# A retention kernel's K and Q: cast by the load, or loaded as fp32 and cast on ScalarE

## The chip, the cores and the metric

The kernel runs on one core of one Trainium2 chip. The metric is the device time of one execution in microseconds (us); lower is better. TensorE is called PE, its weight loads PEld, VectorE DVE, ScalarE ACT, GpSimd POOL and SyncE SP, as in the profile.

## The reference

Two layers run one after the other: a retention layer (attention without softmax, with a decay), and a feed-forward layer with a sigmoid-approximated GELU.

```python
# q, k, v: (8, 8, 576, 64) fp32; w_in (512, 2048), w_out (2048, 512)
scores = q @ k.T / sqrt(64)                        # per batch and head
Dmat   = where(i >= j, gamma_h ** (i - j), 0)      # gamma_h = 1 - 2 ** (-5 - h)
ret    = (scores * Dmat) @ v
x      = ret.transpose(0, 2, 1, 3).reshape(4608, 512)
h      = x @ w_in
out    = (h * sigmoid(1.702 * h)) @ w_out
```

## The kernel before

The 4608 tokens are cut into 36 units of 128 rows (all 8 heads of a unit at once), and four units make a chunk; there are nine chunks, 0 to 8. The last 64 rows of two batches share a unit (8, 17, 26, 35), and the loads of such a unit are two DMAs in place of one.

For each unit the kernel needs four things. Its K and Q rows lie in `kqn` as bf16: the DMA on POOL's queue reads fp32 from memory and writes bf16 (`load_kq`, line 228). The same rows lie transposed in `kqT`, made either by PE with an identity (`transpose_pe`, line 360, and a copy out of PSUM by DVE or ACT, line 376) or by a DMA transpose on SP's queue (`dma_transpose`, line 399). Its V rows lie in `vn` as fp32 (`load_v`, line 244) and are scaled into `vp` as bf16 by DVE or POOL (`scale_v`, line 353). PE then computes the scores from `kqT` (line 501), masks go in on the way out of PSUM (`scores_out`, line 514), and a running K-V state per head is added up (`state_both` and `state_sum`, lines 429 and 442), cast on ACT (`cast_range`, line 459) and used for all earlier rows (`inter`, line 476). `ahead(j)` (line 892) issues the scores and states of units 2j and 2j+1; `block(j)` (line 908) issues the rest of the retention for units 2j and 2j+1 and calls `ahead(j + 1)` in its middle.

The feed-forward layer works chunk by chunk in two stages. The up stage multiplies by w_in and applies the GELU on ACT. The down stage multiplies by w_out. From chunk 1 on the down stage, and from chunk 2 on most of the up stage, uses seven products in place of eight, with sums prepared on DVE (classes `Pair` and `UpSet`). A down stage alternates between two PSUM banks A and B: seven products, each emptied by an ACT copy (line 699) or a DVE addition (line 702), with a hook after each product. The retention of later units is fitted into these hooks and between the up products. In the up stage, the two banks are emptied by GELUs or copies on ACT.

All order is written out by hand. An engine executes its instructions in the order in which the program issues them, and `op` (line 41) adds semaphore waits from the names that an instruction reads and writes. The strings `UP` (line 865) and `DOWN` (line 868) give the order of chunks 3 to 7: in `UP`, `@` starts block(2c+2) and `V` issues four `scale_v` on POOL; in `DOWN`, the parts between bars are the seven hooks, and `c` is the cast of the state. `lead_in` (line 959) is chunk 0; the dictionary `work` in it hangs retention steps behind the steps of chunk 0's down stage, which run in the order (0,0), (1,0), (0,1), ... (1,3), (2,0), ... (3,3). `steady` (line 1080) holds chunks 1 to 8.

Units 0 to 7 are transposed on PE, units 8 to 35 by DMA. The DMA transposes are issued in groups at the start of a chunk, and the loads of later units wait for the last of them:

```python
for u in range(10, 14):
    load(u)
for u in range(8, 14):
    dma_transpose(u, [f"vn{13 % NVN}"])
for u in (14, 15):
    load(u, after=[f"T{13 % NQT}_0"])
```

There are 12 tiles `kqn`, 10 tiles `vn`, and 8 each of `kqT` and `vp`; a unit u uses number u modulo that count.

Of the kernel before, what the change touches and what calls it, by code (L numbers as in the profile page):

```python
# [13 lines left out]
P = 128  # L14
# [146 lines left out]
def bass_retnet_parallel__then__act_gelu_quick_kernel(  # L161
# [7 lines left out]
):  # L169
    NLD, NVN, NVP, NQT, NKV, NST = 12, 10, 8, 8, 16, 4  # L170
    es = ExitStack()
    with es:
# [5 lines left out]
        iota_k = sb("iota_k", [P, 5], FP32)  # L178
        kqn = [sb(f"kqn{i}", [P, 2, H, DH], BF16) for i in range(NLD)]
        vn = [sb(f"vn{i}", [P, H, DH], FP32) for i in range(NVN)]  # L180
        w_in_sb = sb("w_in_sb", [P, 4, FF], BF16)
# [45 lines left out]

        def load_kq(u, which, eng="pool", after=()):
            if which and u in RUNS:
                return load_q_runs(u)  # L230
            sl = u % NLD
            src = (k, q)[which]

            def f(e):
                return [
                    e.dma_start(  # L236
                        kqn[sl][p0 : p0 + n, which, :, :],
                        src[b, :, s0 : s0 + n, :].rearrange("h p d -> p h d"),
                    )
                    for p0, n, b, s0 in unit_rows(u)  # L240
                ]
            op(eng, f, reads=after, writes=[f"kq{sl}_{which}"], dma=f"d_kq{sl}_{which}", ndma=len(unit_rows(u)))

# [534 lines left out]
        class UpSet:  # L778
# [85 lines left out]

        UP = """PE13 00 01 V 10 PK12 11 02 12 03 13 04 14 F0 05 F1 20 06 15 16 21 @ L1 x 22 23 L0 F2
            PX14 s2 24 25 PY15 26 L2 g0-8a s2 g8-16a"""

        DOWN = """s2|c g8-16b|B g0-8b s4||x|X|c s2"""
        last_store = {}
# [61 lines left out]
        def cast_now():  # L931
            now(casts)
            casts.clear()

        def load(u, after=()):
            if u < NU:
                load_kq(u, 0, after=after)
                load_kq(u, 1, after=after)
                load_v(u, after=after)
# [19 lines left out]
        def lead_in():  # L959
# [14 lines left out]
            for i in range(4):  # L974
                load_wout(i)
            for u in range(4, 10):
                load(u)
            op("dve", lambda e: e.memset(warmt.ap(), 0.0), writes=["warm"])
# [56 lines left out]
            up_group(0, 0, 4, 2, 3, "A")  # L1035
            scale_v(3)
            scores(3)
            scores_out(3, 1, 0)
# [13 lines left out]
            for f in range(8, NF):  # L1052
                up(0, f)
            def ahead45():
                ahead(2)
                for u in (4, 5):
                    state_sum(u, 0)
                    state_sum(u, 1)
                state_cast(4, 6)
                scores_out(4, 2, 0)  # L1060
                scores_out(4, 2, 1)

            work = {
                (1, 3): lambda: (scale_v(4), transposes(4, "E", "D", "dve")),
                (2, 0): lambda: (transposes(5, "E", "D", "dve"), scale_v(5)),
                (2, 1): ahead45,
                (3, 1): lambda: now(block(2, lambda: None)),
                (3, 2): lambda: (transposes(6, "C", "D", "dve"), scale_v(6)),
                (3, 3): lambda: (transposes(7, "E", "K", "dve"), scale_v(7)),
            }  # L1070
# [9 lines left out]
        def steady():  # L1080
            four = Pair(0, 2, 2)
            for c in range(1, NCH):
                if c == 1:
                    for u in range(10, 14):
                        load(u)
                    for u in range(8, 14):
                        dma_transpose(u, [f"vn{13 % NVN}"])
                    for u in (14, 15):
                        load(u, after=[f"T{13 % NQT}_0"])
                else:  # L1090
                    for u in range({2: 16, 3: 20}.get(c, 4 * c + 6), min(4 * c + 10, NU)):
                        dma_transpose(u)
                    if c == 2:
                        for u in (16, 17):
                            scale_v(u, "pool")
                    if c == 2 or c == NCH - 1:
                        for u in range(4 * c + 10, 4 * c + 14):
                            load(u, after=[f"T{(4 * c + 9) % NQT}_0"])
                last = c == NCH - 1
                if c == 1:  # L1100
                    for i in range(16):
                        f0, lo = 2 * (i % 8), 2 * (i // 8)
                        up_group(1, f0, 2, lo, lo + 2, turn())
                        if i == 0:
                            ahead(3)
                            now(ahead_out(3, False))
# [13 lines left out]
                        if i == 9:  # L1120
                            winsums(0, 8)
                    for u in (14, 15):
                        dma_transpose(u)
                    for u in (16, 17):
                        load(u, after=[f"T{15 % NQT}_0"])
                else:
# [10 lines left out]
                    def side(w, c=c, sums=sums):  # L1137
# [4 lines left out]
                        elif w[0] == "g":  # L1142
                            sums(*[int(f) for f in w[1:-1].split("-")], which=(0, 1) if w[-1] == "a" else (2, 3))
                        elif w == "c":
                            cast_now()
                        elif w == "X":
                            now(xsums(c + 1))
                        elif 2 * (2 * c + 2 + (w == "B")) < NU:
                            rest.extend(block(2 * c + 2 + (w == "B")))
# [5 lines left out]
                    if wide:  # L1155
                        free = "AB" if turns[0] % 2 else "BA"
                        sets.append(UpSet(c, 2, *free))
                        for w in UP.split():
# [4 lines left out]
                            elif w == "V":  # L1163
                                for u in range(4 * c + 6, min(4 * c + 10, NU)):
                                    scale_v(u, "pool", [sets[0].o])
                                for u in range(4 * c + 10, 4 * c + 14):
                                    load(u, after=[f"T{(4 * c + 9) % NQT}_0"])
                            elif w[0] == "L":
# [5 lines left out]
                    else:  # L1174
                        for n in range(7):
                            for w in sets:
                                w.step(n)
                            if c == 2 and n == 1:
                                now(rest)
                                rest.clear()  # L1180
                            if n in ((3, 4) if c == 2 else (1, 4)):
                                for u in vps[:1]:
                                    scale_v(u)
                                del vps[:1]
                            if c == 2 and n == 4:
                                state_cast(12, 14)
                            if n in (4, 5):
                                for w in sets[:-1] if n == 4 else sets[-1:]:
# [37 lines left out]
                def hook(i):  # L1226
                    if c == 1:
# [18 lines left out]
                        if i == 6:  # L1246
                            rest.extend(block(5, cast=False))
                            now(rest[:2] + xsums(2) + rest[6:])
                            rest[:] = rest[2:6]
                        return  # L1250
                    if wide:
# [10 lines left out]
                    if c == 2 and i == 1:  # L1262
                        for u in (18, 19):
                            dma_transpose(u)
                        for f0, f1 in ((0, 8), (8, 12), (12, 16)):
# [11 lines left out]
                    if i == 5:  # L1277
                        now(rest)
                        rest.clear()

                four.run(c, hook)
# [63 lines left out]
```

## Time and profile before

| | |
|---|---|
| median of 3 runs | 280.83 us (280.28 to 280.91) |
| the profiled execution's own time | 282.98 us |
| its span, first to last instruction | 281.0 us |
| mean granted PE clock | 0.994 |
| PE busy | 268.7 us (96%) |
| DVE busy | 201.4 us (72%) |
| ACT busy | 155.6 us (55%) |
| POOL busy, issue of DMAs included | 130.8 us (47%) |
| DMA queue of POOL, share of 16 engines | 71.2% |
| DMA queue of SP, share of 16 engines | 27.7% |

Busy time is summed within an engine, so engines overlap. A matmul counts as busy until its modelled end, and matmuls are pipelined. Where the profile names an instruction, `out<-in` are the tiles that it writes and reads, with L and a line number of the kernel; an idle time is put down to the instruction whose semaphore came last. A DMA has an issue on a queue, whose length is that of the issue, and a landing, which is counted from the start of the issue. Times inside the execution are counted from the start of the span.

### The profile page before, as it was taken

The numbers are of one execution on the slowest core, as the hardware profiler recorded it, in microseconds if no ns is written. First come the engines' busy times: TensorE is split into PE (matmuls) and PEld (weight loads), VectorE is DVE, ScalarE is ACT, GpSimd is POOL, SyncE is SP. The second block draws the span as 40 slices with busy tenths as digits, with TensorE's granted clock in tenths as the row PEclk, the third lists the DMA queues.
The fourth block names the chain that finished last, engine by engine and source line by source line (L and its number), as shares of the span: only waits on it lengthen the run. The fifth ranks groups of instructions, "written<-read, shape, count | busy, mean of one in ns | idle before, by whom it ended". The sixth has DMA issues, their size and how long they took to land.

```text
span 281.0 us, 9605 instructions
## 1 busy us (share of the span) xinstructions
PE 268.7 (96%) x4242; PEld 210.9 (75%) x4262; DVE 201.4 (72%) x397; ACT 155.6 (55%) x276; POOL 130.8 (47%) x161
## 2 busy tenths in 40 slices
PE   7899999999999999969999999998989999999996
PEld 6576355888877688858977887787778977888585
DVE  5863657598698899639867986796679868866551
ACT  7556433754248733846188608850877178608821
POOL 9999979200344769417738914780347020000000
PEclk9999999999999999979999999999999999999999
DMA  9999999998499979998998989794779070003013
GB/s 159 188 204 207 200 221 249 253 168 152 83 162 223 180 57 162 178 225 100 195 268 97 156 113 249 93 199 65 229 76 149 5 211 16 2 2 150 0 45 106
DMA packets 116937, 40.73 MB, mean 145 GB/s; under 512 B 104096, under 2 KB 110240, under 8 KB 116896
## 3 DMA queue, kind: packets, MB, share of 16 engines
q0 software_dynamic: 79712, 22.82, 71.2%
q1 hardware_dynamic: 36896, 17.05, 27.7%
q8 instruction: 33, 0.54, 0.8%
q10 hardware_dynamic: 288, 0.26, 0.3%
q14 instruction: 8, 0.07, 0.1%
HBM read 36.70 MB, written 9.44 MB: 164 GB/s over the span
## 4 chain that ended last, share of the span: by engine, by line
PE 74%; DMA 10%; POOL 8%; DVE 5%; issue 2%; ACT 1%; POOLq 0%
PE psB L686 17%; PE psA L686 17%; DMA vn<-in_v_dram 6%; DMA kqT<-kqn 4%; PE psX L802 4%; PE psC L802 3%; PE psB L580 3%; PE psA L580 3%; PE psB L802 3%; PE psA L802 3%; POOL w_in_sb L271 3%; PE psY L802 2%; PE psD L802 2%; PE psE L566 2%; PE psK L566 2%
## 5 line engine op out<-in xcount | busy, mean ns | idle before, releaser
L236 POOL DMA_DIRECT2D kqn<-in_k_dram x39 | 34.9, 904 | 45.3 <-DMA kqT<-kqn 43.2
L355 POOL TENSOR_TENSOR vp<-vn,vfac 128x512 bf16<-128x512 f32 x20 | 20.5, 1041 | 54.0 <-DVE part L816 43.0
L249 POOL DMA_DIRECT2D vn<-in_v_dram x40 | 36.7, 929 | 0.1
L236 POOL DMA_DIRECT2D kqn<-in_q_dram x37 | 33.1, 904 | 0.6 <-issue 0.6
L825 ACT ACTIVATE gT<-part 128x512 bf16<-128x512 f32 (+1 forms) x38 | 30.6, 847 | 0.0
L699 ACT ACTIVATE osb<-psA 128x512 f32<-128x512 f32 (+1 forms) x19 | 10.5, 552 | 35.6 <-PE psA L686 35.5
L699 ACT ACTIVATE osb<-psB 128x512 f32<-128x512 f32 (+1 forms) x17 | 9.3, 547 | 33.1 <-PE psB L686 33.1
L460 ACT ACTIVATE kv<-stm 128x1024 bf16<-128x1024 f32 (+1 forms) x17 | 15.3, 901 | 10.7 <-DVE stm L451 10.7
L554 DVE TENSOR_TENSOR xT<-psX,gq 128x512 bf16<-128x512 f32 x16 | 11.0, 689 | 14.0 <-PE psX L529 14.0
L686 PE MATMUL psA<-wsum,gT 128*128 128x256 bf16 x144 | 17.4, 273 | 0.1
L686 PE MATMUL psB<-wsum,part 128*128 128x256 bf16 x128 | 15.6, 273 | 1.0 <-issue 1.0
L686 PE MATMUL psA<-wsum,part 128*128 128x256 bf16 x128 | 15.5, 273 | 0.0
L686 PEld LDWEIGHTS psA<-wsum,gT 128*128 128x128 bf16 x144 | 13.9, 98 | 2.1 <-DVE osb L702 0.4
L686 PE MATMUL psA<-w_out_sb,gT 128*128 128x256 bf16 x128 | 15.4, 273 | 0.0
L686 PE MATMUL psB<-w_out_sb,gT 128*128 128x256 bf16 x128 | 15.4, 273 | 0.0
L668 DVE TENSOR_TENSOR part<-gT 128x1024 bf16<-128x1024 bf16 (+2 forms) x20 | 11.6, 580 | 4.9 <-ACT gT L825 4.3
L580 PE MATMUL psB<-xT,w_in_sb 128*128 128x256 bf16 x112 | 14.6, 273 | 0.0
L686 PEld LDWEIGHTS psB<-wsum,part 128*128 128x128 bf16 x128 | 12.3, 98 | 2.7 <-issue 1.2
L355 DVE TENSOR_TENSOR vp<-vn,vfac 128x512 bf16<-128x512 f32 x16 | 10.6, 685 | 4.7 <-DMA vn<-in_v_dram 4.7
L686 PEld LDWEIGHTS psB<-w_out_sb,gT 128*128 128x128 bf16 x128 | 12.5, 98 | 1.9
L816 DVE TENSOR_TENSOR part<-psY,part 128x512 f32<-128x512 f32 x14 | 9.6, 687 | 5.9 <-ACT part L812 4.0
L580 PE MATMUL psA<-xT,w_in_sb 128*128 128x256 bf16 (+1 forms) x120 | 13.8, 259 | 0.0
(186 smaller groups left out, 749.1 us busy)
## 6 DMA issues: line engine op xcount, KB each, us to landing
vn<-in_v_dram POOLq DMA_DIRECT2D x32, 256.0 KB, 5.7
out_dram<-osb SPq DMA_DIRECT2D x30, 256.0 KB, 2.6
kqn<-in_k_dram POOLq DMA_DIRECT2D x31, 128.0 KB, 5.0
kqn<-in_q_dram POOLq DMA_DIRECT2D x31, 128.0 KB, 5.6
w_out_sb<-in_moe_w_out_dram POOLq DMA_DIRECT2D x4, 512.0 KB, 13.8
out_dram<-osb SPq DMA_DIRECT2D x10, 128.0 KB, 2.3
w_in_sb<-in_moe_w_in_dram POOLq DMA_DIRECT2D x8, 128.0 KB, 5.3
w_in_sb<-in_moe_w_in_dram POOLq DMA_DIRECT2D x4, 256.0 KB, 7.8
```

The lines of the kernel that those rows point to most:

```text
L236: e.dma_start(kqn[sl][p0 : p0 + n, which, :, :], src[b, :, s0 : s0 + n, :].rearrange("h p d -> p h d"),)
L249: e.dma_start(vn[sl][p0 : p0 + n, :, :], v[b, :, s0 : s0 + n, :].rearrange("h p d -> p h d"))
L355: op(eng, lambda e: e.tensor_tensor(vp[u % NVP].ap(), vn[sl].ap(), vfac[:, ty, :, None].to_broadcast([P, H, DH]), ALU.mult), reads=[f"vn{s ...
L460: op("act", lambda e: e.activation(kv[:, i0 % NKV : i0 % NKV + n, :, :], stm[:, i0 % NST : i0 % NST + n, :, :], AF.Copy), reads=[f"stm{(i0 ...
L554: op("dve", lambda e: e.tensor_tensor(xT[ch % 2][:, slice(hh, 4, 2), P * jj : P * jj + 2 * P].rearrange("p g (u t) -> p u g t", u=2), ps32 ...
L566: op("pe", lambda e, a=a: e.matmul(bank[b][:, n0:n1], w_in_sb[:, a, P * f : P * f + P], xT[c % 2][:, a, n0:n1], start=(a == 0), stop=(a == ...
L580: op("pe", lambda e, a=a, f=f, i=i: e.matmul(bank[b][:, n * i : n * i + n], w_in_sb[:, a, P * f : P * f + P], xT[c % 2][:, a, P * lo : P * ...
L668: op("dve", lambda e, d=d, x=x, y=y, alu=alu: e.tensor_tensor(d, x, y, alu), reads=kx + ky, writes=kd)
L686: op("pe", lambda e, x=x, y=y, t=t, s=not more and t == 0 and k == 0, z=k == NF // 2 - 1: e.matmul(bank[b][:, 256 * t : 256 * t + 256], x, ...
L699: op("act", lambda e: e.activation(dst[0], src[0], AF.Copy), reads=src[1], writes=dst[1])
L802: op("pe", lambda e, x=x, y=y, i=i, s=not more and i == 0 and k == 0, z=k == 1: e.matmul(bank[b][:, 256 * i : 256 * i + 256], x, y, start= ...
L825: op("act", lambda e: e.activation(dst, src, AF.Gelu_apprx_sigmoid), reads=reads, writes=[f"g_{f0 + 2 * i + q}_{j}" for i in range(2) for ...
```

## The change

K and Q of units 4 to 35 are loaded as fp32 into four staging tiles `stage`, still on POOL's queue, and a new `cast_kq` casts them on ACT into `kqn`. Units 0 to 3 stay as they were. Except for units 4 and 5, which PE still transposes, each cast issues the unit's DMA transpose right behind itself, so units 6 and 7 are now transposed by DMA too, and no group of DMA transposes is left. With the staging tiles, `kqn` shrinks from 12 to 8 tiles and `vn` from 10 to 6. K and Q loads and V loads of one unit are issued apart from each other at many places, and no load waits for a DMA transpose any more; a K or Q load waits for the cast that empties its staging tile. In chunk 0, `ahead45` moves from behind step (2,1) to behind (2,2), and in chunk 1 `ahead(3)` moves from behind the first of 16 `up_group`s to behind the second. In chunks 3 to 7 the casts of the next chunk but one's units stand at the hooks (`k1` to `k4`), and the loads stand in the up stage (`l1`, `l2`, `v`); `l1` has a wait for the DVE instruction issued last before it.

```diff
-    NLD, NVN, NVP, NQT, NKV, NST = 12, 10, 8, 8, 16, 4
+    NLD, NVN, NSG, NVP, NQT, NKV, NST = 8, 6, 4, 8, 8, 16, 4
...
+        stage = [sb(f"stage{i}", [P, 2, H, DH], FP32) for i in range(NSG)]
...
-        def load_kq(u, which, eng="pool", after=()):
+        def load_kq(u, which, eng="pool", after=(), gate=()):
...
-            sl = u % NLD
             src = (k, q)[which]
+            if u < 4:
+                dst, key = kqn[u], f"kq{u}_{which}"
+            else:
+                dst, key = stage[u % NSG], f"sg{u % NSG}_{which}"
...
+        def cast_kq(u, which=(0, 1), on_pe=False):
+            if u >= NU:
+                return
+            n = slice(which[0], which[-1] + 1)
+            op("act", lambda e: e.activation(kqn[u % NLD][:, n, :, :], stage[u % NSG][:, n, :, :], AF.Copy),
+               reads=[f"sg{u % NSG}_{i}" for i in which], writes=[f"kq{u % NLD}_{i}" for i in which])
+            if which[-1] and not on_pe:
+                dma_transpose(u)
...
-        UP = """PE13 00 01 V 10 PK12 11 02 12 03 13 04 14 F0 05 F1 20 06 15 16 21 @ L1 x 22 23 L0 F2
+        UP = """PE13 l1 00 01 V 10 PK12 11 02 12 l2 v 03 13 04 14 F0 05 F1 20 06 15 16 21 @ L1 x 22 23 L0 F2
...
-        DOWN = """s2|c g8-16b|B g0-8b s4||x|X|c s2"""
+        DOWN = """s2|c g8-16b k1|k2 B g0-8b s4|k3|x k4|X|c s2"""
...
+        def loads(u, gate=()):
+            if u < NU:
+                load_kq(u, 0, gate=gate)
+                load_kq(u, 1, gate=gate)
...
-            for u in range(4, 10):
-                load(u)
+            load(4)
+            load(5)
+            for u in (6, 7):
+                loads(u)
...
+            for u in range(6, 10):
+                load_v(u)
...
-                (1, 3): lambda: (scale_v(4), transposes(4, "E", "D", "dve")),
-                (2, 0): lambda: (transposes(5, "E", "D", "dve"), scale_v(5)),
-                (2, 1): ahead45,
+                (1, 3): lambda: (scale_v(4), load_v(10), cast_kq(4, on_pe=True), loads(8)),
+                (2, 0): lambda: (cast_kq(5, on_pe=True), loads(9), transposes(4, "E", "D", "dve")),
+                (2, 1): lambda: (transposes(5, "E", "D", "dve"), scale_v(5), load_v(11)),
+                (2, 2): lambda: (cast_kq(6), loads(10), cast_kq(7), loads(11), ahead45()),
                 (3, 1): lambda: now(block(2, lambda: None)),
-                (3, 2): lambda: (transposes(6, "C", "D", "dve"), scale_v(6)),
-                (3, 3): lambda: (transposes(7, "E", "K", "dve"), scale_v(7)),
+                (3, 2): lambda: (scale_v(6), load_v(12)),
+                (3, 3): lambda: (scale_v(7), load_v(13)),
...
+            HOOK1 = ((12,), (13,), (), (14,), (15,), (16,), ())
+            CASTS = (3, 4, 7, 8, 11, 12)
...
-                if c == 1:
-                    for u in range(10, 14):
-                        load(u)
-                    for u in range(8, 14):
-                        dma_transpose(u, [f"vn{13 % NVN}"])
-                    for u in (14, 15):
-                        load(u, after=[f"T{13 % NQT}_0"])
-                else:
-                    for u in range({2: 16, 3: 20}.get(c, 4 * c + 6), min(4 * c + 10, NU)):
-                        dma_transpose(u)
...
-                        if i == 0:
+                        if i == 1:
                             ahead(3)
                             now(ahead_out(3, False))
...
+                        if i == 0:
+                            cast_kq(8)
+                            loads(12)
+                        if i in CASTS:
+                            cast_kq(9 + CASTS.index(i) // 2, (CASTS.index(i) % 2,))
+                        if i == CASTS[1]:
+                            loads(13)
+                    for u in range(14, 16):
+                        load(u)
...
+                            elif w[0] == "l":
+                                for u in range(4 * c + 8 + 2 * int(w[1]), 4 * c + 10 + 2 * int(w[1])):
+                                    loads(u, [pr.streams["dve"][-1]] if w == "l1" else ())
+                            elif w == "v":
+                                for u in range(4 * c + 10, min(4 * c + 14, NU)):
+                                    load_v(u)
...
                             if c == 2 and n == 1:
                                 now(rest)
                                 rest.clear()
+                                cast_kq(17)
+                                for u in (16, 17):
+                                    scale_v(u, "pool", [sets[0].o])
+                                load(18)
+                                load(19)
...
                             if c == 2 and n == 4:
                                 state_cast(12, 14)
+                                load(20)
+                                load(21)
...
+                    if c == 2 and i in (1, 2, 3, 4):
+                        cast_kq(17 + i)
```

`range(6, 10)` stands in `lead_in` behind `scale_v(3)`. `HOOK1` holds the units that chunk 1's seven hooks cast, `CASTS` the up_groups of chunk 1 that are followed by half a cast (K or Q) of units 9 to 11. In chunk 1's hooks the casts of units 12 and 13 are followed by the loads of K and Q of units 16 and 17, and the cast of 13 also by the V loads of 16 and 17.

## The prediction

> **What bounds the kernel now.** I read the page's busy shares and slices first, then the waits, then the stretches of the trace stage by stage.
>
> ```profile
> PE 268.7 (96%) x4242; PEld 210.9 (75%) x4262; DVE 201.4 (72%) x397; ACT 155.6 (55%) x276; POOL 130.8 (47%) x161
> ...
> PEclk9999999999999999979999999999999999999999
> DMA  9999999998499979998998989794779070003013
> ```
>
> PE is busy 96% of 281.0 us: the kernel is its matmul stream, and time is won or lost only where that stream shrinks or stands still. DMA is loaded in the first 150 us. One clock slice is low, about 119 to 126 us. The list of waits has one PE wait of size, and the stretches show what it cost (stretch, length, busy PE, PEld, DVE, ACT, POOL, granted clock, DMA share, GB/s):
>
> ```profile
> PE psC L507 <- DMA kqT<-kqn: 2.0, 1, 2.0
> ```
> ```profile
> 110.43:127.83 17.40, 15.15 (x227) 11.69 (x227) 10.20 (x19) 11.96 (x21) 6.23 (x7) 0.90 1.40 180
> 141.51:155.53 14.02, 13.88 (x227) 10.73 (x227) 9.83 (x18) 12.69 (x22) 9.36 (x12) 1.00 0.93 180
> 169.21:182.82 13.61, 13.55 (x210) 10.57 (x211) 9.07 (x16) 12.57 (x22) 8.65 (x10) 1.00 0.91 177
> ```
> ```profile
> 121.67:125.08 3.41, 3.04 (x73) 2.43 (x75) 2.05 (x4) 0.93 (x2) 1.04 (x1) 0.50 1.18 272
> ```
>
> The three stretches are the same stage, the up products of chunks 3, 4 and 5. In chunk 3 the scores of unit 19 (L507) stand 2.03 us for a transposed kqT; then the granted clock is 0.50 for 3.41 us. The stage is 3.4 to 3.8 us longer than its sisters: 2.0 of standing, some 1.5 of slow clock.
>
> The Trainium skill, "TensorE: Matmul & The Clock Gate", section "Why this matters for your kernels", allows idle gaps up to about 3 us before the clock is halved. By that rule the gap is worth 2.0 us, and the sum below would be 1.5 us smaller; here 2.03 us of standing was followed by 0.50, so the trace disagrees and I go by it.
>
> **The change, part by part.** Profiled execution: span 281.0, own time 282.98 us, 2.15 above the median of 280.83. Differences are summed on its trace and taken off the median.
>
> *Removed: TensorE transposes of units 6 and 7.*
>
> ```profile
> 47.67 0.39 PE L371 MATMUL psC<-ident,kqn 128*128 128x128 bf16 x4
> 47.90 0.39 PE L371 MATMUL psD<-ident,kqn 128*128 128x128 bf16 x4
> 48.12 1.03 PE L592 MATMUL psB<-w_out_sb,gT 128*128 128x512 bf16 x4
> ```
>
> Unit 6 holds PE from 47.67 to 48.12, 0.45 us; unit 7 the same (48.98 to 49.43). **-0.9 us.** Their four copies were on DVE and ACT beside it.
>
> *Removed: the late unit 19.* Before, its loads wait for earlier transposes, and its own transpose is issued at 111.4 among other loads. After, it is loaded during chunk 2's up stage, cast at hook 2 of chunk 2's down stage (about 102) and transposed then; PE wants it at 119.8. Even the worst landing below, 11.0, gives 114. **-3.5 us** (3.4 to 3.8).
>
> *Loads.* K and Q stay on POOL's queue at 0.9 us of issue each. Unit 4's Q lands 37.7, its V 38.5, unit 5's K 39.3: cast or not, a load takes 0.75 to 0.87 us of a full queue. **0**, bounds -0.5 to +0.5. Staging tiles come free with each cast, so POOL's next load waits for it, and behind it wait POOL's own vp scalings; they are wanted 10 us later. In chunks 3 to 7 the first two units' loads also wait for a DVE operation of the up stage and stand ahead of those scalings: 4 x 0.9 = 3.6 us of issue in a stretch where POOL so far waited 6 to 13 us for DVE's part (L816), **0**.
>
> *Added: 32 casts on ACT*, priced by the like-shaped copy, with ACT's row in a down stage:
>
> ```profile
> L460 ACT ACTIVATE kv<-stm 128x1024 bf16<-128x1024 f32 x11 | 11.6, 1051 | 6.8 <-DVE stm L451 6.8
> ```
> ```profile
> 157.97 1.05 ACT L460 ACTIVATE kv<-stm 128x1024 bf16<-128x1024 f32 x1
> 160.97 0.60 ACT L699 ACTIVATE osb<-psB 128x512 f32<-128x512 f32 x1 [1.95 <-PE psB L686]
> 163.96 0.60 ACT L699 ACTIVATE osb<-psA 128x512 f32<-128x512 f32 x1 [2.39 <-PE psA L686]
> 169.19 0.60 ACT L699 ACTIVATE osb<-psB 128x512 f32<-128x512 f32 x1 [4.64 <-PE psB L686]
> ```
>
> 32 x 1.05 = 34 us, ACT to some 190 busy. In the down stages it idles 2 to 4.6 us between copies and one cast per hook fits, so nothing is late there. Without that cover, a copy up to 1.05 us late eats the 1.75 us that PE spends on the other bank, still 0. Queued behind a cast whose load is late are gelus and bank copies, for which PE waits two products later. Two crowded places: unit 17's cast in chunk 2's up stage (ACT 12.03 busy of 15.30), and units 14 to 16 queued behind the state cast at 77.5, which push the last bank copy from 80.1 to about 81.4 while PE wants that bank at 82.4. **+0.3 us**, 0 to 1.5.
>
> *Chunk 0's down stage.* The copy of unit 4's Q (ACT) now queues behind unit 5's cast (Q lands 40.1, cast to 41.1), and unit 5's PE transposes need both that cast and bank D emptied by that copy (41.7): PE, there at 40.9, starts late and ends about 0.5 late. **+0.5**, 0 to 1.0.
>
> *Added: DMA transposes of units 6 and 7.* Unit 6's Q lands at 26.4 + 16.1 = 42.5:
>
> ```profile
> L236 POOL DMA_DIRECT2D kqn<-in_q_dram x1: 1054/1054/1054, 26.4 to 26.4; - x1
> DMA to landing us min/median/max: 16.1/16.1/16.1
> ```
>
> Its cast ends 43.5. Unit 7's Q moves up one place (its V comes later), to about 44.1; its cast ends 45.1, and SP, free of unit 6's 1.26 us of issue, starts its transpose. Nothing but stores queues behind on SP. PE gets to the scores of units 6 and 7 (ahead(3), now after the second up_group) at 49.43 - 0.9 + 0.5 + two groups of 0.9 = about 50.9. Two answers for the DMA transposes, among loads and alone:
>
> ```profile
> L401 SPq DMA_TRANSPOSE kqT<-kqn x1: 1237/1237/1237, 107.6 to 107.6; - x1
> DMA to landing us min/median/max: 6.7/6.7/6.7
> ...
> L401 SPq DMA_TRANSPOSE kqT<-kqn x1: 1233/1233/1233, 111.4 to 111.4; - x1
> DMA to landing us min/median/max: 10.4/10.4/10.4
> ...
> L401 SPq DMA_TRANSPOSE kqT<-kqn x4: 1256/1261/1305, 143.0 to 147.1; - x4
> DMA to landing us min/median/max: 2.8/3.1/3.7
> ```
>
> Alone 3.1; sent into a load stream 7.0 (80.3), 6.7 (94.1), 6.7 (107.6), then 10.4, 11.0, 5.6 in the thick of chunk 2 and 3. Stores in this very stretch took 5.5 to 6.1 against 2.4 to 3.1 alone, 3 us more, which points to the lower group: I take 7.0. Unit 7 lands at 52.1: **+1.2 us** of standing, too short to cost clock (less than the 2.03 that did). Bounds: 5.6 lands at 50.7, 0; 10.4 lands at 55.5, 4.6 of standing plus 1.5 of clock, +6.1.
>
> Sum: -0.9 - 3.5 + 0.3 + 0.5 + 1.2 = **-2.4 us: 278.4** (span about 278.6). No more comes out, because PE's other waits are each 1.0 us or less.
>
> **The rivals.**
>
> *A, slower: unit 7 lands as late as unit 19 did.* For it: 10.4 and 11.0 were the second and third transposes sent under a load stream, and from 36 to some 54 us loads are queued without a break. Against: firsts took 6.7 to 7.0, and here two are sent 1.6 us apart. With 6.1 in place of 1.2: +2.5, 283.3. Counting the clock, it decides against the change once standing passes 2.1 us (2.1 + 1.5 = 3.6 against the 3.6 won elsewhere), a landing after 53.0.
>
> *B: each 256-byte packet of the transpose waits for a whole load packet.* A transpose is 1024 packets of 256 bytes, 64 per DMA engine at 18 ns; an fp32 load goes in 4096-byte packets of 172 ns (V's, median), where the cast loads showed 128-byte ones of 32. 64 x 190 ns = 12.2 us per transpose; unit 7 would land only when the loads run dry, about 55, plus 2: 57, 6.1 standing plus 1.5 clock in place of 1.2: +4.0, 284.8. Against: in the trace one 256-byte packet rarely waits for a 4096-byte one; at 97 us 542 of them passed in the microsecond in which 32 did. The Trainium skill, "DMA: Bandwidth & Descriptors", section "Queues, rings and completion order", has the engines take turns between queues by whole packets, which speaks for B.
>
> *C: ACT becomes the bound.* If each of seven down stages lost 0.35 us behind casts: +2.4, so 0: 280.8. Against: the idle rows above.
>
> *D, more: unit 7 in time (-1.2), and chunk 6's up stage (14.66 before) comes down to its sisters' 13.61 with the transposes spread (-1.0).* -4.6, 276.2.
>
> That the change does not do what it says: the loads are not what PE waits for, so cheaper ones alone give 0; the gain hangs on unit 19's new place.
>
> **How the numbers follow.** A measurement here can tell 0.2%, 0.56 us. Forecast (landing up to 52.7): 0.52, all faster. D: 0.12, faster. A: 0.20, of which 0.02 near zero. B: 0.05, slower. C with other ACT delays: 0.11, split 0.02 faster, 0.05 same, 0.04 slower. Faster 0.66, same 0.07, slower 0.27. The range runs from D, 276.2, to just short of A's end, 283.0, and leaves out B and the tail of A.
>
> **What would show it.** Right: no L507 wait in chunk 3, that stage 13.6 to 14.0 us, the clock at 1.0 there; one PE wait for kqT near 51 us of about 1 us. Wrong: that wait over 2 us with a 0.50 clock behind it (A or B), or ACT's copies in the down stages no longer waiting for PE (C).

## The result, and the profile after

The changed kernel takes 298.15 us, the median of 4 runs (295.60 to 301.97), against 280.55 us for the kernel before (279.86 to 280.91) on the same chip. The ratio is 1.054, with a 95% interval of 1.050 to 1.058; it is lower than the quotient of the medians because it leaves out the two slower runs of the changed kernel (300.55 and 301.97 us), which lie over 1.5% above its fastest. By that ratio it is 15 us slower, where 2.4 us faster was forecast. The profile below is of a second execution, 294.81 us, with a span of 293.2 us. The first profiled one, 300.55 us, shows the same two waits, 13.5 and 6.0 us long.

From the page after: busy shares, and the rows of the granted clock and of DMA.

```profile
PE 268.6 (92%) x4226; PEld 210.3 (72%) x4246; DVE 200.8 (68%) x395; ACT 184.0 (63%) x309; POOL 130.0 (44%) x161
...
PEclk9999999657999999999999999999999999999999
DMA  9999999993798969975878489769762340003013
```

PE's work hardly changed, and ACT grew by the casts. The low clock slice of before (the 18th) is gone, and three slices, from 51 to 73 us, are low instead. The list of PE's waits, the stretches of the up stages of chunks 1, 3, 4 and 5, the stretch at half clock, and the two DMA transposes behind it (columns as before):

```profile
PE psC L520 <- DMA kqT<-kqn: 15.6, 2, 12.3
```
```profile
48.87:82.63 33.76, 18.10 (x257) 14.08 (x256) 12.55 (x22) 13.98 (x25) 10.01 (x13) 0.75 0.88 179
128.04:141.78 13.74, 13.68 (x226) 10.68 (x227) 10.20 (x19) 11.85 (x21) 11.22 (x13) 1.00 0.64 190
155.56:169.40 13.84, 13.78 (x226) 10.73 (x227) 9.82 (x18) 12.57 (x22) 11.95 (x14) 1.00 0.63 190
183.18:196.79 13.61, 13.54 (x210) 10.57 (x211) 9.07 (x16) 12.58 (x22) 11.69 (x13) 1.00 0.69 199
```
```profile
53.21:70.28 17.07, 3.93 (x77) 2.97 (x78) 2.44 (x6) 0.79 (x2) 1.48 (x2) 0.50 1.03 169
```
```profile
L414 SPq DMA_TRANSPOSE kqT<-kqn x2: 1349/6678/12008, 43.3 to 44.9; - x2
...
DMA to landing us min/median/max: 19.8/20.8/21.8
```

Chunk 3's up stage is 13.74 us where it was 17.40, as forecast. Chunk 1's is 33.76 us where it was 16.04. There the scores of units 6 and 7 stand 12.3 and 3.2 us for their transposes, sent at 43.3 and 44.9 and landed 19.8 and 21.8 us later; from 53.21 us on, 2.4 us into the first wait, the clock is 0.50 for 17.07 us. The second transpose also held SP for 12.01 us of issue where one alone takes 1.25. All other stages together come out 2 us shorter than before (chunk 0's down stage -0.5, chunk 5's down stage -1.2, chunk 6's up stage -0.8, the rest small; in the last two PE stood 1.00 and 0.73 us before, for nothing that the profile names, and does not after), so chunk 1's stage is the loss: +17.7 - 3.7 - 2 = +12, and the spans differ by 12.2.

Why the transposes took so long is in the count of packets of each queue (POOL's is q0, SP's q1), for 50 to 53 us and for 60 to 66 us of the kernel after:

```profile
q0 software_dynamic: 277, 0.91, 94.0%
q1 hardware_dynamic: 277, 0.07, 11.8%
```
```profile
q1 hardware_dynamic: 805, 0.26, 77.1%
q0 software_dynamic: 105, 0.35, 36.0%
```

In the first stretch 277 packets of the loads pass and 277 of the transposes: one for one. Nearly all the time goes to the load packets (most of them 4096 bytes at 0.19 us). At 92 packets a microsecond the 1024 packets of one transpose need 11 us; the first 1024 passed from 47.8 to 58.2 us, and the second 1024 until 66.2. That is rival B's mechanism. In the second stretch the loads no longer fill their queue, but the transposes' queue passes only 134 packets a microsecond, where it passes 598 in the first microsecond without loads (67 to 68 us): 0.61 MB in 6 us, 102 GB/s where the loads alone move 340.

### The profile page after: what moved, and what is told of

Read it like the earlier page. It is cut to its first block, busy times and chain, and to the rows that moved or that the text cites. A ratio compares the mean times of both kernels' runs of the same rounds, so it can differ in the third digit from the quotient of the medians.

```text
span 299.0 us, 9603 instructions
## 1 busy us (share of the span) xinstructions
PE 269.8 (90%) x4226; PEld 210.9 (71%) x4246; DVE 200.7 (67%) x395; ACT 184.0 (62%) x309; POOL 130.2 (44%) x161
## 4 chain that ended last, share of the span: by engine, by line
PE 81%; DMA 11%; DVE 4%; issue 1%; ACT 1%; POOL 1%; POOLq 0%; DVEq 0%
PE psA L699 16%; PE psB L699 16%; DMA kqT<-kqn 9%; PE psB L593 4%; PE psA L593 4%; PE psX L815 4%; PE psC L815 4%; PE psY L815 3%; PE psB L815 3%; PE psD L815 3%; PE psA L815 3%; DMA vn<-in_v_dram 2%; PE psA L579 2%; PE psK L579 2%; PE psB L579 2%; PE psA L605 2%
## 5 line engine op out<-in xcount | busy, mean ns | idle before, releaser
L240 POOL DMA_DIRECT2D stage<-in_k_dram x36 | 31.2, 866 | 82.6 <-DVE pm L529 36.6
L262 POOL DMA_DIRECT2D vn<-in_v_dram x40 | 34.6, 885 | 6.6 <-DVE wsum L646 5.7
L252 ACT ACTIVATE kqn<-stage 128x1024 bf16<-128x1024 f32 (+1 forms) x35 | 33.5, 975 | 0.0
L240 POOL DMA_DIRECT2D stage<-in_q_dram x36 | 30.9, 860 | 0.2
L520 PE MATMUL psC<-kqT 64*64 64x64 bf16 x288 | 8.8, 197 | 19.5 <-DMA kqT<-kqn 19.5
L598 ACT ACTIVATE gT<-psA 128x512 bf16<-128x512 f32 (+1 forms) x14 | 7.9, 564 | 25.8 <-PE psA L593 25.6
L464 DVE TENSOR_TENSOR stm<-psK,stm 128x256 f32<-128x256 f32 x21 | 8.7, 416 | 22.0 <-PE psE L449 21.8
L520 PEld LDWEIGHTS psC<-kqT 64*64 64x64 bf16 x288 | 6.8, 109 | 22.1 <-DMA kqT<-kqn 19.9
L699 PE MATMUL psA<-wsum,part 128*128 128x256 bf16 x128 | 15.5, 273 | 0.0
L699 PE MATMUL psB<-wsum,part 128*128 128x256 bf16 x128 | 15.5, 273 | 0.0
L593 PE MATMUL psB<-xT,w_in_sb 128*128 128x256 bf16 x112 | 15.4, 284 | 0.0
```

The lines of the kernel that those rows point to most:

```text
L240: e.dma_start(dst[p0 : p0 + n, which, :, :], src[b, :, s0 : s0 + n, :].rearrange("h p d -> p h d"),)
L252: op("act", lambda e: e.activation(kqn[u % NLD][:, n, :, :], stage[u % NSG][:, n, :, :], AF.Copy), reads=[f"sg{u % NSG}_{i}" for i in whic ...
L262: e.dma_start(vn[sl][p0 : p0 + n, :, :], v[b, :, s0 : s0 + n, :].rearrange("h p d -> p h d"))
L520: op("pe", lambda e, hp=hp, a=a, hh=hh: e.matmul(ps32(SB[hh])[64 * a : 64 * a + 64, c0 + 64 * hp : c0 + 64 * hp + 64], qt[64 * hh : 64 * h ...
L593: op("pe", lambda e, a=a, f=f, i=i: e.matmul(bank[b][:, n * i : n * i + n], w_in_sb[:, a, P * f : P * f + P], xT[c % 2][:, a, P * lo : P * ...
L699: op("pe", lambda e, x=x, y=y, t=t, s=not more and t == 0 and k == 0, z=k == NF // 2 - 1: e.matmul(bank[b][:, 256 * t : 256 * t + 256], x, ...
```

## The experiments

Two theories stood at first. P, the prediction's reading with a worse price: only units 6 and 7, sent by DMA in the middle of chunk 0's loads, are late. M, formed after the first four runs: any DMA transpose in flight beside queued loads is slow and slows them, and the waits that the change took away (transposes behind the last load, loads behind the last transpose) had kept the two apart. Rivals to M were S, that the staging itself costs the time, and, for the packets, P in a new sense, that only 4096-byte packets matter.

**Units 6 and 7 back on PE, in the changed kernel.**

```diff
-                (2, 2): lambda: (cast_kq(6), loads(10), cast_kq(7), loads(11), ahead45()),
+                (2, 2): lambda: (cast_kq(6, on_pe=True), loads(10), cast_kq(7, on_pe=True), loads(11), ahead45()),
...
+                (3, 2): lambda: (transposes(6, "C", "D", "dve"), scale_v(6), load_v(12)),
+                (3, 3): lambda: (transposes(7, "E", "K", "dve"), scale_v(7), load_v(13)),
```

> The changed kernel with the transposes of units 6 and 7 put back on TensorE, in their old places; staging, ACT casts and all loads as changed. Theory P (the time is lost because the two early DMA transposes creep among 4096-byte load packets): the two PE waits at L520 (13.5 and 5.9 us) and the 20.5 us of half clock are gone, and the rest of the change shows alone: 16 transposes back on PE (+0.9), unit 19 no longer late (-3.5 to -3.7): 276.5 to 278. Rival A (staging and the 32 casts on ACT cost time of their own): the waits are gone but the time stays above 280.5.

302.22 us, ratio 1.074 [1.065, 1.083]. The waits did not go; they moved to the next transposes, those of units 8 to 11.

```profile
PE psC L520 <- DMA kqT<-kqn: 10.6, 3, 5.2
```
```profile
L414 SPq DMA_TRANSPOSE kqT<-kqn x4: 1237/4746/12498, 53.2 to 74.7; - x4
...
DMA to landing us min/median/max: 12.6/20.0/25.5
```

P fell: units 6 and 7 are only the first transposes to meet the loads.

**Units 6 and 7 by DMA, in the kernel before.** Its loads cast on the way; the two transposes are issued behind step (2,1) of chunk 0's down stage, and `ahead(3)` comes one `up_group` later.

```diff
-                (2, 1): ahead45,
+                (2, 1): lambda: (dma_transpose(6), dma_transpose(7), ahead45()),
```

> The kernel before with one part of the change alone: units 6 and 7 transposed by DMA (issued behind their loads, scores one up_group later), while all K and Q loads stay cast by the DMA in 128-byte packets. Theory P (a 256-byte transpose packet takes turns with one load packet, so the size of the load packets counts): two thirds of the load packets are now 32 ns instead of 194 ns, unit 7 is issued at about 46.5, lands after 8 to 11 us, PE stands 4 to 7 us: 283 to 289. Rival Q (any queue of loads starves a transpose, whatever its packets): landing 20 us or more after issue, PE stands 15 to 20 us: 295 or more. Rival R (the old loads do not hinder it): under 282.

286.17 and 290.55 us in two runs, against 280.87. In the profile, of the run of 290.55 us, the transposes landed 9.7 and 12.9 us after issue, and PE waited for them for 7.3 us in all. So cast loads hold transposes up too, only about half as long as fp32 loads.

**The loads behind units 6 and 7 held.** In the changed kernel the loads of K and Q of units 8 to 11, and of V from unit 10 on, wait for unit 7's transpose; casts come later in chunk 1.

```diff
+            def held():
+                load_kq(8, 0, after=["T7_0"])
+                load_kq(8, 1)
+                load_v(10)
+                ...
-                (2, 2): lambda: (cast_kq(6), loads(10), cast_kq(7), loads(11), ahead45()),
+                (2, 2): lambda: (cast_kq(6), cast_kq(7), held(), ahead45()),
```

> The changed kernel, but the loads of K and Q of units 8 to 11 and of V of units 10 to 13 wait on POOL until unit 7's DMA transpose has landed (their casts in chunk 1 stand a few up_groups later). Theory P: once the V loads queued before have run dry at about 47, units 6 and 7 land at 49 to 51, PE hardly waits (0 to 1 us), no half clock: 276 to 278.5. Rival S (a DMA transpose in this stretch is slow by itself, or is held up by the loads already queued ahead of it): it lands after 55, PE stands 4 us or more, over 282.

293.67 us, ratio 1.046 [1.036, 1.056]. Units 6 and 7 now landed 6.1 and 4.8 us after issue, in time. The loss had moved on again:

```profile
PE psA L593 <- ACT gT L598: 5.4, 2, 4.7
PE psC L520 <- DMA kqT<-kqn: 3.6, 1, 3.6
```

The first is PE waiting for a GELU that stands on ACT behind a cast whose load comes late; the second is for unit 9, whose transpose took 20.1 us among the held loads (unit 8's took 9.7).

**K and Q of units 8 to 11 loaded from ACT's queue,** where the same fp32 loads go in 256-byte packets.

```diff
-                (2, 0): lambda: (cast_kq(5, on_pe=True), loads(9), transposes(4, "E", "D", "dve")),
+                (2, 0): lambda: (cast_kq(5, on_pe=True), loads_act(9), transposes(4, "E", "D", "dve")),
```

> The changed kernel with the K and Q loads of units 8 to 11 issued from ACT's queue instead of POOL's, which puts the same bytes in 256-byte packets beside the transposes; V loads stay on POOL. Theory P: the transposes take turns with packets of their own size, units 6 and 7 land within 7 to 11 us of their issue and PE stands 2 to 6 us in place of 19.5, while ACT's own issues cost 1 to 3 us: 280 to 286. Rival Q (bytes queued count, not packets): unit 7 lands 20 us or more after its issue and the time stays at 294 or more.

291.0 us, the median of two runs, ratio 1.037 [1.029, 1.045]. The transposes of units 6 to 9 landed fast:

```profile
DMA to landing us min/median/max: 4.6/5.6/6.0
```
```profile
PE psE L384 <- ACT kqn L252: 6.2, 1, 6.2
PE psD L384 <- ACT kqT L397: 3.6, 1, 3.6
```

No PE wait for a DMA transpose was left. ACT paid instead: its issues of loads stood for 3.8 and 2.8 us, with unit 5's cast and a copy of unit 4's transposes behind them on ACT, and PE's transposes of unit 5 behind these.

**The staging kept, transposes and loads apart.** Units 6 and 7 on PE, as in the first experiment; in chunk 1 the waits of the kernel before put back around the changed kernel's casts and loads, with the transposes and the casts of units 12 to 16 moved to suit.

```diff
+                    for u in range(8, 14):
+                        dma_transpose(u, ["sg1_1", "vn1"])
+                    load(14, after=["T5_0"])
+                    for u in (15, 16, 17):
+                        load(u)
```

> The changed kernel's staging, casts and loads, with units 6 and 7 transposed on TensorE, and in chunk 1 the transposes of units 8 to 13 held until the Q load of unit 13 and V of unit 13 have landed, the loads of units 14 to 17 until the transpose of unit 13 has landed. Theory M (a DMA transpose in flight beside queued loads slows both; before, waits kept the two apart): no PE wait for kqT over 1 us in chunk 1, transposes land 2.7 to 5 us after issue there, 276.5 to 280 us. Rival S (the staging itself costs the time: 4096-byte packets, or casts on ACT that wait for late loads and hold up gelus and copies): 288 us or more, with PE waiting for ACT.

285.26 us, ratio 1.011 [1.007, 1.016]. The six transposes of chunk 1:

```profile
L414 SPq DMA_TRANSPOSE kqT<-kqn x6: 1298/1312/2582, 63.4 to 71.5; - x6
...
DMA to landing us min/median/max: 2.8/2.9/4.6
```

There is no wait for a transpose and no half clock in this execution. About four fifths of the loss is gone ((1.054 - 1.011) / 0.054), with fp32 staging and all 32 casts in place: M holds against S for the bulk. The nearest run without the waits is that with units 6 and 7 on PE, 1.074. The time is above M's 276.5 to 280, so S has a part. Chunk 1's and 2's up stages show it:

```profile
51.06:68.45 17.39, 16.62 (x259) 12.83 (x257) 12.67 (x22) 15.03 (x28) 5.28 (x6) 1.00 0.92 243
84.50:101.16 16.66, 15.36 (x232) 10.41 (x225) 13.13 (x26) 14.48 (x24) 10.82 (x14) 1.00 1.03 264
```

ACT is busy 15.03 of 17.39 us in the one and 14.48 of 16.66 in the other (before: 10.75 of 16.04 and 12.03 of 15.30), each stage is 1.35 us longer. PE's small waits there, 0.7 and 1.2 us, are for ACT; what makes up the rest was not found. Chunk 0's down stage has two more, 0.67 us (unit 5's cast) and 0.72 us (the state's cast behind those of units 6 and 7). Three stops from 153 to 212 us, 1.1 to 1.3 us each, are put down to "issue" and not to ACT; the kernel before has two, 1.0 and 0.7 us.

**The kernel before without its waits.** Cast loads, no staging; only the waits between loads and transposes are taken out of chunk 1.

```diff
-                        dma_transpose(u, [f"vn{13 % NVN}"])
+                        dma_transpose(u)
...
-                        load(u, after=[f"T{13 % NQT}_0"])
+                        load(u)
```

> The kernel before with its cast loads and no fp32 staging, without the waits that keep loads and transposes apart in chunk 1 (the transposes of units 8 to 13 no longer wait for V of unit 13, the loads of units 14 to 17 no longer for transposes). Theory M: transposes take 10 us or more, PE waits for kqT in chunk 1, 284 us or more. Rival P (only 4096-byte packets hold up a transpose): transposes land within 7 us, 279.5 to 282.

293.08 us, the median of two runs, ratio 1.040 [1.030, 1.049]. The transposes of units 8 to 13 landed 10.8 to 15.5 us after issue where they took 2.7 to 4.4, and loads beside them up to 37 us after issue, where the slowest in this place had taken 14. Chunk 1's up stage is 2.2 us longer than before, and its down stage 10.3 (before, then this run):

```profile
65.47:81.50 16.03, 15.80 (x410) 13.47 (x409) 11.91 (x22) 4.67 (x7) 5.29 (x6) 1.00 0.88 135
69.20:95.53 26.33, 18.11 (x410) 14.63 (x409) 11.91 (x21) 4.67 (x7) 0.27 (x1) 0.87 1.80 131
```
```profile
PE psA L686 <- issue: 5.4, 1, 5.4
PE psA L580 <- issue: 2.0, 1, 2.0
```

This is the other half of the evidence: with neither fp32 loads of K and Q nor casts on ACT (V is fp32 in both kernels), taking the waits away costs 4%. Only 1.1 us of it is a wait for kqT, so most of the loss does not reach PE by the road that M named. The larger stops are put down to "issue", nothing that the list of waits names; 6.83 us of half clock begin in the longer one. The DMA view for 84 to 86 us holds one packet of another queue:

```profile
q8 instruction: 1, 0.02, 4.5%
```

It is 16 KB long and passes from 84.06 to 85.52 us; PE goes on at 87.01. The packet of this queue before the shorter stop's end passes until 66.83, and PE goes on at 68.21. In the twelve profiles of whole kernels there are 16 stops of PE over 0.6 us put down to "issue", and each ends 1.2 to 1.5 us after such a packet. So PE most likely stood there for its own instructions. That they came late because loads and transposes crowded the DMA engines is a guess; no run tests it. (This profile also has a wait of 1.8 us for w_in at 14 us, with 3.41 us of half clock, which is not of this change.)

**Loads and transposes alone.** Two kernels without the computation; of the first, the packets in single microseconds. Cast loads alone (50 to 51 us) and with transposes (54 to 55), fp32 loads behind a backlog with transposes (106 to 107), and fp32 loads without a backlog with transposes (163 to 164):

> No computation at all, zeros are stored: only loads and DMA transposes, in seven phases with a barrier after each. Phases 1 to 4: four w_out loads as a backlog, then 12 K or Q loads; 1 cast loads alone, 2 the same with two transposes issued when the last w_out load has landed, 3 fp32 loads alone, 4 fp32 loads with two transposes. Phases 5 to 7 without the w_out loads, so that POOL's issue (0.9 us) sets the pace: 5 cast loads with two transposes, 6 fp32 loads with two, 7 fp32 loads with four. Theory M: in 2 and 4 the transposes land 12 us or more after issue and the loads take 5 us or more longer than in 1 and 3; in 5 to 7 they land within 7 us. Rival P (packet size): in 2 they land within 7 us and cost the loads under 2 us, in 4 they take 12 us or more.

```profile
q0 software_dynamic: 1225, 0.15, 242.5%
```
```profile
q1 hardware_dynamic: 418, 0.10, 80.1%
q0 software_dynamic: 416, 0.05, 79.9%
```
```profile
q0 software_dynamic: 97, 0.31, 93.2%
q1 hardware_dynamic: 99, 0.03, 11.6%
```
```profile
q1 hardware_dynamic: 166, 0.04, 52.4%
q0 software_dynamic: 21, 0.07, 44.4%
```

With a backlog of loads, packets pass one for one, 418 to 416 and 99 to 97. Who pays depends on their sizes. With cast loads two transposes landed after 7.5 and 9.5 us and delayed the last load by 3.6 us. With fp32 loads behind a backlog they landed after 10.1 and 9.7 us, just behind the last load, and delayed the loads by only 0.6 us. So neither M's 12 us nor P's limit of 7 us was met. Without a backlog M's 7 us was wrong too: with cast loads two transposes took 6.5 and 8.4 us, with fp32 loads two took 8.1 and 11.2, four 6.2 to 15.3, and the last of the fp32 loads came some 5 and 9 us later than in a phase of the second kernel without transposes. There the one-for-one rule fails too: 21 load packets and 166 transpose packets passed in a microsecond where 84 packets of 4096 bytes pass alone, and these took 0.3 to 0.9 us each, by the mean of a microsecond, against 0.19. Why both slow down there stays open.

> No computation, zeros are stored; 12 K or Q loads a phase, transposes issued when the second load has landed (in phase 7: the last of four w_out loads). 1 to 3: fp32 loads from ACT's queue with 0, 2 and 4 transposes; 4 and 5: fp32 and cast loads from POOL's queue alone; 6: cast loads from POOL with four transposes; 7: fp32 loads from POOL behind a backlog with four. Theory by packets (each packet of a transpose takes turns with one packet of a load): with 256-byte load packets from ACT's queue transposes land within 6 us; in 6 four take 15 us in all and the loads lose 6 to 8 us; in 7 none lands until the loads have run dry, and the loads lose under 1.5 us. Rival (the number of transposes in flight decides): phase 3 shows 10 us or more as well.

From ACT's queue fp32 loads let two transposes land after 6.3 and 6.8 us and four after 5.9 to 6.8, a little over the 6 us expected; the loads lost 2.7 and 4.1 us. Four beside cast loads took 6.4 to 9.2 us each and cost the loads 5.8 us. Behind a backlog of fp32 loads from POOL the four landed at 132.7 to 135.3 us, the last load at 131.9: none before the loads had run dry. The count of transposes alone does not decide; the packets they alternate with do.

**The late unit 19, in the kernel before.** Two orders in which the loads of units 20 and 21 come behind unit 19's transpose instead of ahead of it; the second also puts POOL's scalings of units 18 and 19 ahead of those loads.

```diff
-                        for u in range(4 * c + 10, 4 * c + 14):
-                            load(u, after=[f"T{(4 * c + 9) % NQT}_0"])
+                    if c == 2:
+                        for u in (18, 19):
+                            load_kq(u, 0, after=[f"T{17 % NQT}_0"])
+                            load_kq(u, 1)
...
+                        for u in (20, 21):
+                            load_kq(u, 0, after=[f"T{19 % NQT}_0"])
```

> The kernel before with one order changed: the loads of units 20 and 21 wait for the transpose of unit 19 instead of standing ahead of it. Theory M: the transpose of unit 19 lands before 115 us, the 2.0 us PE wait of chunk 3 and its 3.4 us of half clock go, its up stage comes to 13.7 to 14.2 us, 277.0 to 278.5 in all. Rival (the wait only moves to units 20 and 21, whose loads now come some 10 us later): 280 to 282.

283.31 us against 282.0, ratio 1.004 [0.999, 1.008]. Unit 19 landed at 114.8, in time, but PE then stood for POOL's scalings, and half the clock went for 3.41 us as before:

```profile
PE psK L436 <- POOL vp L355: 2.5, 2, 1.8
```

> The kernel before with one order changed as in the earlier run that held the loads of units 20 and 21 behind the transpose of unit 19, but now with POOL's scalings of units 18 and 19 ahead of those loads, so that they aren't late. Theory M: no PE wait over 1 us in chunk 3, no half clock there, its up stage 13.6 to 14.2 us in place of 17.4, 277.0 to 278.5 us. Rival (units 20 and 21 become the late ones): a PE wait of 1.5 us or more in chunk 3's down stage, 279.5 to 281.

280.71 us against 279.48, ratio 1.0036 [1.0001, 1.0071]: not faster, although in its profile the stall is gone.

```profile
110.35:124.09 13.74, 13.68 (x226) 10.70 (x227) 10.19 (x19) 11.85 (x21) 7.39 (x8) 1.00 1.30 195
```

The up stage is 13.74 us in place of 17.40, and the span 278.4 in place of 281.0, a gain of 2.6 us between two profiles that the timed runs do not have. They tell why: 3.41 us at half clock in a span of 281 us make a mean clock of 0.994, and 15 of the 17 timed runs of the kernel before in this comparison have 0.999 or 1.000. Their spans have a median of 277.5 us, 3.5 below the 281.0 of the profile, about as much as the late unit 19 costs there. In all three comparisons that list the clock of the kernel before it is 35 runs of 43. The late unit 19 with its half clock is not in them. And the new order has a stall of its own, near what its rival priced (1.5 us or more, 279.5 to 281), though in chunk 4's up stage in place of chunk 3's down stage: unit 23's transpose, sent at 142.0 us before the last load beside it had landed (143.4), lands 6.8 us after issue.

```profile
PE psC L507 <- DMA kqT<-kqn: 1.6, 1, 1.6
```
```profile
137.93:153.43 15.50, 13.88 (x227) 10.80 (x228) 9.83 (x18) 12.58 (x22) 6.72 (x9) 1.00 1.15 177
```

That stage took 14.02 us before; the clock stays at 1.00.

**Both kernels profiled once more, unchanged.**

> The kernel before, unchanged, profiled a second time, since nearly all of its runs in the comparisons have a mean granted clock of 1.000 and the first profiled execution had 0.994. Theory V (the late unit 19 belongs to that one execution): no half-clock record, the up stage of chunk 3 at 13.6 to 14.5 us, the span 277 to 279 us. Rival (it is in every execution, and only the clock record is missing): that stage at 15.5 us or more.

282.49 us, mean clock 0.994, and the stall of unit 19 once more, 1.9 us with 3.41 us of half clock behind it. So theory V fell as put: it is not one odd execution. Both full profiles of the kernel before have the stall and are 2 to 3 us above the timed medians, while most timed runs cannot have its half clock. Whether recording the profile makes that transpose late was not tried.

> The changed kernel, unchanged, profiled a second time. Both theories expect the same two waits for kqT in chunk 1, 15 us or more together, and a span of 293 to 300 us; what it tells is how much the place of the waits moves between executions.

This is the execution shown above, 294.81 us, with waits of 12.3 and 3.2 us, in the same places as the first.

## Why the prediction was wrong

*The term that failed: "+1.2 us" for the DMA transposes of units 6 and 7, with unit 7 taken to land 7.0 us after issue.* It landed after 21.8 us, PE stood 15.6 us and the clock was at half speed for 17.07 us: +17.7 us in that stage. Even the bound of +6.1 was a third of it. The times around it were right: unit 7's transpose was sent at 44.95 us against 45.1 forecast, and PE came for unit 6 at 50.8 against 50.9. Only the landing was wrong. The six durations it was picked from, 5.6 to 11.0 us, had been measured under another load. The view of DMA issues tells the two apart, for 91 to 97 us and for 40 to 48 us of the kernel before:

```profile
kqn<-in_k_dram POOLq DMA_DIRECT2D x2, 64.0 KB, 3.9
kqn<-in_q_dram POOLq DMA_DIRECT2D x2, 64.0 KB, 3.5
kqT<-kqn SPq DMA_TRANSPOSE x2, 5.6
```
```profile
kqn<-in_k_dram POOLq DMA_DIRECT2D x3, 128.0 KB, 13.7
kqn<-in_q_dram POOLq DMA_DIRECT2D x3, 128.0 KB, 13.4
```

At 91 to 97 us a load lands some 4 us after its issue, little more than the 3.4 us of one sent alone in the kernel of loads, so hardly anything is queued ahead of it. At 40 to 48 us it lands after 13.5 us: 15 to 18 loads are on their way at a time. The price taken, 7.0 us, is of 80.3 us, where loads landed 3.7 to 5.4 us after issue; around the rows of 10.4 and 11.0 us they took 5.7 to 11.1. So the price of a transpose in a full queue was taken from a nearly empty one. The prediction quoted the 16.1 us of unit 6's own Q load and used it only to date the cast.

*Rival B had the mechanism and got 0.05.* It was set aside because "at 97 us 542 of them passed in the microsecond in which 32 did" (the view has 548 and 33). That microsecond belongs to the short queue: 32 load packets are well under the 84 that a full queue passes. The Trainium skill, "DMA: Bandwidth & Descriptors", section "Queues, rings and completion order", says that the DMA engines switch between queues at whole packets; 277 to 277 agrees with it. B's time was too low as well: it let the loads run dry at 55 us and put 6.1 us on the wait. In the changed kernel loads up to unit 12's stood in the same queue, and they passed until 66 us.

*"Loads: 0".* The change part by part spoke of issue slots and of bytes, and put no price on the waits that the change takes away, though the loads after transposes and transposes after loads stood in the listing. The kernel before without them costs 4.0% and the staging with them 1.1%: those waits were the largest thing in the diff, though in the kernel before the loss showed mostly as stops for "issue".

*The base: "-3.5 us" for unit 19, "taken off the median".* The mechanism was right: no wait there, the stage 13.74 us, the clock 1.0, -3.66 between the profiles. But the sum was made on an execution of 282.98 us and taken off a median of 280.83. By their clocks and spans most timed runs do not have the stall, and the 2.15 us between the two is a good part of it. Had all else come out as forecast, -2.4 on the profiled execution would have been 280.6 us, near zero against the timed runs.

*"+0.3" and "+0.5" for ACT.* In the changed kernel the casts hide in the stall. In the version with the staging kept and the transposes apart they show: the two waits of 0.67 and 0.72 us in chunk 0's down stage against +0.5, and 1.35 us in each of two crowded up stages against +0.3. So these three stages lost about 4 us there, in part by where that version put the casts; only some 3.3 us of it are waits named for ACT. The claim for the down stages held: ACT's copies still wait for PE, the longest 4.6 us, so rival C was no part of it.

*"-0.9" for PE's transposes* was right in size: chunk 0's down stage came out 0.53 us shorter, against -0.9 + 0.5 of the two terms in it. Rival D's -1.0 in chunk 6's up stage came too, -0.83, but by luck: what is gone there is the 0.73 us stop for "issue", and not a wait for a transpose.

Of the signs that were named, that for unit 19 came, and the one for A or B: a wait over 2 us near 51 us with a 0.50 clock.

## What to carry to other kernels

Before pricing a DMA from like rows, compare how deep the queue beside it is: the landing time of the loads issued around it says that, 4 us here for an empty queue and 13.5 us for a full one, and, as long as loads are queued without a break, packet counts of one for one give the time (1024 packets at 92 a microsecond). A wait that holds a transfer back can be what makes it fast, so a change that takes such waits away has to be priced for what then travels together. And set the sum on the same kind of execution as the median: a stall seen in a profile that runs 2 us over the timed runs may not be there to be won.

## What was not expected of the hardware

A DMA transpose and loads in large packets can slow each other far below what either moves alone. Between 60 and 66 us the kernel after moved 102 GB/s and the kernel that only moves data moved 112 in the microsecond shown, where fp32 loads alone moved 340. Loads of the same bytes from ACT's queue, in 256-byte packets, let four transposes land within 6.8 us. An issue on SP can stand: 12.01 us for one transpose that takes 1.25 us to issue alone. And a stop that the profile puts down to "issue" can be looked up among the DMA packets: all 16 here ended 1.2 to 1.5 us after a 16 KB packet of the queue named "instruction".
